# Moving part of batch 1's transposes from TensorE to DMA in an attention and SwiGLU kernel on one core

## The chip, the core and the metric

The program runs on one core of a Trainium2 chip. The core has TensorE for matmuls (PE in the profile, with PEld for its weight loads), VectorE (DVE), ScalarE (ACT), GpSimd (POOL), SyncE (SP) and 16 DMA engines that all of its transfers share. The metric is the device time of one execution in microseconds; less is better.

## The reference

Attention with squared ReLU in place of softmax over 8 batches of 12 heads (448 tokens, head size 64), then a token-wise RMS norm and a SwiGLU layer (768 to 1536 to 768) over all 3584 tokens:

```python
scores = q @ k.transpose(0, 1, 3, 2) / sqrt(64)
attn   = maximum(scores, 0) ** 2 / 448 @ v
x      = attn.transpose(0, 2, 1, 3).reshape(3584, 768)
xn     = x / sqrt(mean(x * x, axis=-1) + 1e-6) * rms_g
g      = xn @ w_gate
out    = (g * sigmoid(g) * (xn @ w_val)) @ w_out
```

Inputs and output are float32 in HBM; the kernel converts to bf16 in the loads and accumulates in float32.

## The kernel before

The kernel writes out its instruction order itself. While the program is built, a small planner (`Planner`) keeps a clock for every engine, gives each operation an assumed cost, and emits the operation that can start first; ties go by a rank. On the chip every engine then runs its instructions in that fixed order and waits on semaphores where data isn't there. The assumed costs change only the order.

**Loads.** GpSimd issues them in the order q and k of batch 0, v of batch 0, four slices each of `w_gate` and `w_val`, q, k and v of batch 1 (each in halves of six heads), two halves of `w_out`, then q and k of batch 2. At most eight of them are in flight: the ninth waits for the first.

**Heads to columns.** Scores need q and k with the head dimension on the partitions (`qkT`, six pairs of heads j = 0 to 5). For batches 0 and 1 (`PE_T = 2`) TensorE transposes them through PSUM (`transposes`, L419 and L427; 16 matmuls for a pair of batch 1) and VectorE copies the result to `qkT` (L437). For batch 2 and later VectorE sorts each chunk of q and k by head (L326) and SyncE issues eight DMA transposes (`transpose_dma`, L339).

**Attention.** For each pair of heads there are score products into PSUM (L483, L501, L519), ReLU on ACT or DVE (L467, L465), a square on DVE (L470), and then, for two pairs at a time, the products with v (L605). ACT scales the result into `xT` (L653). For the norm, DVE squares `xT` and adds into a float32 sum (L668, L670), closes it to one bf16 tile (L674), and one TensorE product with a matrix of ones sums over partitions. ACT makes the reciprocal root with Ln and Exp (L728, L732), which needs another function table than Silu does (L390 loads one), and DVE scales `xT` to `xn` (six instructions, L737). Batch 0 runs in two halves of 224 tokens; its last pairs of heads are already squared by ACT straight from PSUM (L656).

**Stream.** All products of the feed-forward layer go through `Stream.step` (L872). The array is used as two halves of 64 rows: a slot holds one matmul on the upper half for one group (its lead) and one on the lower half for another (its follow). A slot in which only one half has work lasts as long. The feed-forward of one batch (gate and value, `gv`, then the output projection, `o`) is mixed with the attention of the next but one, batch 0's with that of batch 1. When there is no follow, a rule looks for another group to lead so that the pair is full; it holds for batches 1 to 6 only.

**Head.** In the first 26 us, in which data arrives and batch 0's attention runs, the planner puts products on zeros into TensorE's gaps (`fill`, L1147; in the trace the first of these follow each other in 0.187 us, from 8.9 us on in about 0.1). A gap is filled if it is at least 0.3 us long by the plan, up to 0.15 us before its end.

Of the kernel before, what the change touches and what calls it, by code (L numbers as in the profile page):

```python
# [9 lines left out]
BF16 = mybir.dt.bfloat16  # L10
# [56 lines left out]
class Planner:  # L67
# [84 lines left out]
    def run(self, until):  # L152
        while not until():
# [8 lines left out]
            if e == "PE" and self.fill is not None:  # L162
                self.fill(self.free["PE"], t)
            if op == "step":
# [8 lines left out]
def kernel(  # L173
# [104 lines left out]
    def load(nm, b, h0=0, h1=H, deps=()):  # L278
        src = src_of[nm][b, h0:h1]
        if (nm, b) == ("k", 0):  # L280

            def runs_of_seven():
                nc.gpsimd.dma_start(  # L283
                    out=wo_sb[:D, h0:h1, :S], in_=src.rearrange("h (p u) d -> p h (u d)", p=D)
                )

            ops = [pool_dma(0.7, D * U * D * 4 * (h1 - h0) / 1e3, 300.0 if h1 == 2 else 340.0, runs_of_seven, deps)]
            landed.setdefault((nm, b), {}).update({h: ops for h in range(h0, h1)})
            return
# [5 lines left out]
        for prt, n, u0, u1 in parts:  # L295
# [12 lines left out]

            ops.append(pool_dma(0.72, kb, (300.0 if h1 == 2 else 340.0) if b == 0 else 400.0, whole, deps))
        landed.setdefault((nm, b), {}).update({h: ops for h in range(h0, h1)})  # L310
# [5 lines left out]

    def transpose_dma(b, deps, seen):

        jobs = [("k", c) for c in range(UH)] + [("q", c) for c in range(NCH)]
        turned[b] = []  # L320
        sorts = []
        for nm, c in jobs:

            def sort(op, nm=nm, c=c):
                n = (P if c < UH - 1 else D) if nm == "k" else PC
                nc.vector.tensor_copy(  # L326
                    out=sorted_of[nm, b][:n, c, :].rearrange("p (h d) -> p h d", d=D),
                    in_=ld[nm, b][:n, :, c * D : (c + 1) * D],
                )

            sorts.append(add(Op({"DVE": 0.06 + H * D * 0.53e-3}, sort, landed[nm, b][0] + list(seen), rank=6)))
        for nm, c in jobs:

            def turn(op, nm=nm, c=c):
                if b not in qkT:
# [3 lines left out]
                op.ins = nc.sync.dma_start_transpose(  # L339
                    out=qkT[b][:, :, 0 if nm == "k" else 1, at : at + n], in_=sorted_of[nm, b][:n, c, :]  # L340
                ).ins

            need = list(deps) + sorts
            turned[b].append(add(Op({"SP": 0.1}, turn, need, ends=arrives(170, 120.0))))

# [14 lines left out]
    def load_wo(s, n):  # L360
        w = FT // n
        w_in["o", s] = pool_dma(0.85, 2360, 400.0, lambda: nc.gpsimd.dma_start(
            out=wo_sb[:, s * w : (s + 1) * w, :],
# [213 lines left out]
    def attend(b, j, lo, w, due):  # L577
# [40 lines left out]
        def fn(op):  # L618
            op.ps = one.ps
            products(False, op.ps.tile)  # L620
            if b == 0 and j == HP - 2:

                ev = add(Op({"DVE": 0.07 + 2 * w * 1.042e-3}, evict, [op], rank=-1))
                sq = add(Op({"ACT": 0.05 + 2 * w * 0.833e-3}, square_ps, [op], rank=-1))
                plan.take(op.ps.banks, [ev, sq])
                squared[lo, j] = sq
            else:
                ev = add(Op({"ACT": 0.05 + 2 * w * 0.833e-3}, evict, [op], rank=1))
                plan.take(op.ps.banks, [ev])
            if b == 0 and j == HP - 2:  # L630
                pass
# [3 lines left out]
            else:  # L635
                cost = (0.08 + 2 * w * 1.042e-3) * (2 if j else 1)
                sq = add(Op({"DVE": cost}, square, [ev], rank=2))
            if j == HP - 2 and b == 0:
                summed[b, lo] = sq
# [15 lines left out]
        def square_ps(op):  # L655
            nc.scalar.activation(  # L656
                out=xn_of[1][:, j : j + 2, lo : lo + w], in_=me.ps.tile[:, :, :w], func=ACT.Square, scale=inv_attn
            )
# [30 lines left out]

    summed, squared, used = {}, {}, []  # L690

# [67 lines left out]
    class Stream:  # L759
# [14 lines left out]
        def options(self, half, taken):  # L774
            here = self.at[half]
            order = [g for g in self.open if g.n == 1]
            order += ([here] if here in self.open and here.count[half] % KT else []) + self.open
# [21 lines left out]
        def step(self, t):  # L799
            lead = self.pick(0, None, t)  # L800
            follow = self.pick(1, lead, t)
            if lead is not None and follow is None and lead.note and 0 < lead.note[0] < B - 1:

# [124 lines left out]

    def norm_sums(b, lo, w):
        return Group(  # L930
            1, w, lambda i: ones_bf[:], lambda i: accs[b, lo][1][:, :w],
            lambda g: norm_scale(b, lo, w, g), "psSS", lambda i: [Later(summed, (b, lo))],
            False,
        )
# [152 lines left out]
    EARLY = 4  # L1087

    def half_scores(lo, j, due):
        for jj in range(2):  # L1090
# [18 lines left out]
    def attention_full(b):  # L1109
# [4 lines left out]
        for j in range(0, HP, 2):  # L1114
            if b < PE_T:
                transposes(b, j)
# [16 lines left out]

    def fill(t0, t1):
        if not fill_on[0] or t1 - t0 < 0.3:
            return
        s = None
        for x in single[::-1]:
# [19 lines left out]
    for s in range(NSL):  # L1158
        load_w("g", s)
        load_w("v", s)  # L1160
    for nm in ("q", "k", "v"):
        load(nm, 1, 0, 6)
        load(nm, 1, 6, 12)
    load_wo(0, 2)
# [4 lines left out]
    for b in range(B):  # L1169
        groups = ffn(b)  # L1170
        if b == 0:
            stream.add(groups[:24])
            plan.run(lambda: first.end.done < NEVER)
            end_head()
            attention_half(HS)
            attention_full(1)
            stream.add(groups[24:])
# [5 lines left out]
        if b + 2 < B:  # L1183
# [10 lines left out]
            attention_full(b + 2)  # L1194
        if 0 < b < B - 1:
            ready_for_norm(b)
# [41 lines left out]
```

## Time and profile before

| | us |
|---|---|
| Median of three runs (lowest, highest) | 441.63 (439.43, 444.19) |
| The profiled execution | 438.65 |
| Its span in the trace | 436.9 |
| Batch 0's first feed-forward product starts | 26.13 |
| Batch 1's first transpose on TensorE starts | 48.29 |
| Batch 0's first output-projection product starts | 71.76 |
| Batch 1's first gate product starts | 85.96 |
| Batch 2's first score product starts | 94.96 |

A row of the trace gives the start, the time that the group took, the engine, the line of the kernel and the tiles. The profile counts TensorE as busy from the first start to the last end of overlapping matmuls, so a busy TensorE can still run half-empty slots.

### The profile page before, as it was taken

What the parts mean: (1) busy time and instruction counts of PE and PEld (TensorE: products, weight loads), DVE (VectorE), ACT (ScalarE), POOL (GpSimd) and SP (SyncE); (2) the same over time, 40 slices, a digit from 0 to 9 for tenths busy, and PEclk for the clock granted to TensorE, in tenths of its full rate; (3) what the DMA queues carried; (4) which work ended last, traced back from release to release, by engine and by line L of the source; (5) the groups of instructions that cost most, each with busy time, mean ns of one, the idle gap of its engine ahead of it and who ended that gap; (6) DMA issues with size and microseconds to landing.
All of it is one profiled execution on the core that took longest, in us unless ns stands there. A gap on an engine that the chain in (4) does not pass through costs nothing.

```text
span 436.9 us, 17119 instructions
## 1 busy us (share of the span) xinstructions
PE 430.4 (99%) x7836; PEld 350.8 (80%) x7836; DVE 255.6 (59%) x461; ACT 263.9 (60%) x391; POOL 47.1 (11%) x67
## 2 busy tenths in 40 slices
PE   8999999999999999999999999999999999999996
PEld 5577876778778777789978997789988997688865
DVE  2987588638945774685757465676655456432210
ACT  3982496649846765775748665586757666342222
POOL 8522400012012001201200012001000000000000
PEclk9999999999999999999999999999999999999999
DMA  8999995799569747886952999089001300030013
GB/s 105 196 204 202 202 205 74 123 187 119 82 94 165 148 96 96 110 154 121 123 77 74 133 144 125 13 141 159 7 2 47 102 4 3 2 91 22 3 38 110
DMA packets 82680, 44.75 MB, mean 102 GB/s; under 512 B 41904, under 2 KB 79152, under 8 KB 82608
## 3 DMA queue, kind: packets, MB, share of 16 engines
q0 software_dynamic: 43232, 24.38, 41.3%
q1 hardware_dynamic: 38992, 18.94, 21.1%
q8 instruction: 61, 1.00, 0.9%
q10 hardware_dynamic: 384, 0.34, 0.3%
q14 instruction: 11, 0.09, 0.1%
HBM read 48.76 MB, written 11.01 MB: 137 GB/s over the span
## 4 chain that ended last, share of the span: by engine, by line
PE 95%; ACT 1%; DMA 1%; DVE 1%; issue 1%; POOL 0%; POOLq 0%
PE psP L872 77%; PE psS L605 8%; PE psS L483 6%; PE psS L519 1%; DMA wo_sb<-in_k_dram 1%; PE psP L427 1%; PE psS L501 1%; PE psP L1147 1%; ACT r L467 1%; PE psP L419 0%; POOL qb L299 0%; DVE hT L957 0%; PE psP L920 0%; ACT qkT L439 0%; POOL wo_sb L283 0%
## 5 line engine op out<-in xcount | busy, mean ns | idle before, releaser
L872 PE MATMUL psP<-xn,wg_sb 64*64 64x448 bf16 (+1 forms) x2304 | 235.1, 338 | 0.2 <-ACT sil L943 0.2
L872 PE MATMUL psP<-xn,wv_sb 64*64 64x448 bf16 (+1 forms) x2304 | 218.5, 338 | 0.1
L467 ACT ACTIVATE r<-psS 128x896 bf16<-128x896 f32 (+1 forms) x162 | 143.6, 922 | 53.5 <-PE psS L483 28.4
L872 PEld LDWEIGHTS <-wg_sb 64*64 64x64 bf16 (+1 forms) x2304 | 132.3, 105 | 17.5 <-issue 3.0
L872 PEld LDWEIGHTS <-wv_sb 64*64 64x64 bf16 (+1 forms) x2304 | 132.6, 105 | 16.3 <-issue 3.3
L872 PE MATMUL psP<-wo_sb,hT 64*128 64x384 bf16 (+2 forms) x1562 | 139.6, 321 | 0.0
L470 DVE TENSOR_TENSOR r<-r 128x896 bf16<-128x896 bf16 (+1 forms) x165 | 98.7, 616 | 58.7 <-ACT r L467 57.9
L872 PEld LDWEIGHTS <-hT 64*128 64x128 bf16 (+1 forms) x1562 | 100.1, 97 | 23.4 <-issue 3.2
L957 DVE TENSOR_TENSOR hT<-sil,psP 128x448 bf16<-128x448 bf16 (+1 forms) x108 | 61.0, 565 | 58.3 <-PE psP L872 44.5
L943 ACT ACTIVATE sil<-psP 128x448 bf16<-128x448 f32 (+1 forms) x108 | 54.9, 508 | 59.7 <-PE psP L872 55.9
L1017 ACT COPY ost<-psP 128x384 f32<-128x384 f32 (+1 forms) x55 | 25.9, 475 | 43.3 <-PE psP L872 42.8
L483 PE MATMUL psS<-qkT 64*64 64x448 bf16 (+1 forms) x420 | 48.2, 350 | 0.0
L605 PE MATMUL psS<-r,vb 64*64 64x448 bf16 (+1 forms) x716 | 43.7, 335 | 0.3 <-PE psS L605 0.2
L737 DVE SCALAR_TENSOR_TENSOR xn<-xT,g_sb,rstd 128x448 bf16<-128x448 bf16 (+1 forms) x54 | 30.2, 628 | 22.2 <-ACT rstd L732 22.1
L299 POOL DMA_DIRECT2D vb<-in_v_dram x20 | 14.3, 736 | 197.0 <-PE psP L872 189.4
L605 PEld LDWEIGHTS <-vb 64*64 64x64 bf16 x756 | 26.1, 106 | 8.4 <-issue 2.0
L653 ACT ACTIVATE xT<-psS 128x896 bf16<-128x896 f32 (+1 forms) x25 | 21.4, 857 | 9.9 <-PE psS L605 9.9
L483 PEld LDWEIGHTS <-qkT 64*64 64x64 bf16 (+1 forms) x420 | 22.0, 103 | 4.6 <-issue 0.7
L390 ACT ACT_TABLE_LOAD x16 | 20.5, 1283 | 1.0 <-PEq L1222 0.7
L668 DVE TENSOR_TENSOR x<-xT 128x896 f32<-128x896 bf16 x14 | 15.2, 1087 | 3.6 <-ACT xT L653 3.6
L670 DVE TENSOR_TENSOR acc<-acc,x 128x896 f32<-128x896 f32 x14 | 15.3, 1092 | 0.5
L299 POOL DMA_DIRECT2D qb<-in_q_dram x12 | 10.2, 854 | 41.7 <-DVE hT L957 13.0
(61 smaller groups left out, 154.6 us busy)
## 6 DMA issues: line engine op xcount, KB each, us to landing
vb<-in_v_dram POOLq DMA_DIRECT2D x12, 384.0 KB, 6.9
qb<-in_q_dram POOLq DMA_DIRECT2D x6, 672.0 KB, 8.1
out_dram<-ost SPq DMA_DIRECT2D x7, 336.0 KB, 3.0
wg_sb<-in_moe_w_gate_dram POOLq DMA_DIRECT2D x4, 576.0 KB, 15.7
wv_sb<-in_moe_w_val_dram POOLq DMA_DIRECT2D x4, 576.0 KB, 17.3
wo_sb<-in_moe_w_out_dram POOLq DMA_DIRECT2D x2, 1152.0 KB, 14.0
kb<-in_k_dram POOLq DMA_DIRECT2D x6, 384.0 KB, 9.8
out_dram<-ost SPq DMA_DIRECT2D x8, 288.0 KB, 3.2
```

The costliest lines, as they stand in the source:

```text
L299: dma = nc.gpsimd.dma_start(out=stage(nm, b)[prt, h0:h1, : (u1 - u0) * D], in_=src.rearrange("h (p u) d -> p h (u d)", p=n)[:, :, u0 * D : ...
L390: nc.scalar.add_instruction(mybir.InstLoadActFuncSet(name=name, act_func_set_id=n, ins=[], outs=[]))
L467: nc.scalar.activation(out=op.view, in_=src, func=ACT.Relu)
L470: nc.vector.tensor_tensor(out=rl.view, in0=rl.view, in1=rl.view, op=ALU.mult)
L483: nc.tensor.matmul(out=ps[m0:m1, hh, :S], lhsT=qkT[b][prt, j, 0, c * P + m0 : c * P + m1], rhs=qkT[b][prt, j, 1, :], start=True, stop=True,)
L605: mm = nc.tensor.matmul(out=ps[hh * D : (hh + 1) * D, jj, :w], lhsT=vb[prt, 2 * (j + jj) + hh, u * D : (u + 1) * D], rhs=r[prt, hh, :], st ...
L653: nc.scalar.mul(out=to, in_=src, mul=inv_attn)
L737: nc.vector.scalar_tensor_tensor(out=xns[b][:, kt, lo : lo + w], in0=xTs[b][:, kt, lo : lo + w], scalar=g_sb[:, kt : kt + 1], in1=rstd[:, ...
L872: mm = nc.tensor.matmul(out=self.ps[m0:m1, : self.w], lhsT=self.lhsT(i)[prt, m0:m1], rhs=self.rhs(i)[prt], start=(half == 0 and i == 0), s ...
L943: nc.scalar.activation(out=s[:, :w], in_=g.ps[:, :w], func=ACT.Silu)
L957: nc.vector.tensor_tensor(out=hT[:, fb, o : o + w], in0=sil[b, fb, lo][1][:, :w], in1=g.ps[:, :w], op=ALU.mult,)
L1017: nc.scalar.copy(out=to, in_=g.ps[:, :w])
```

## The change

Six things change:

1. Of batch 1, heads 8 to 11 of q and k are loaded first, then heads 0 to 3 and 4 to 7. VectorE sorts heads 8 to 11 into a part of `hT` that isn't used yet, and SyncE issues eight DMA transposes for them. TensorE no longer transposes the pairs j = 4 and 5 of batch 1 (32 matmuls), and VectorE no longer copies them out of PSUM.
2. Batch 1's norm is closed after the second two pairs of heads. The last four heads are squared by ACT from PSUM, VectorE takes over their scaling, and the sum over partitions is three products instead of one.
3. The rule for fuller slots also holds in batch 0's output projection.
4. The function table for Ln and Exp is loaded ahead of batch 1's norm, as it already is for later batches.
5. In the head, between 5.5 and 20 us of the plan's clock, a gap is filled from 0.15 us on, and the fill runs up to 0.05 us short of the planned end, or 0.35 us beyond it ahead of transposes.
6. The planner assumes a lower transfer rate for q and k of batch 0's heads 4 to 7 and for `w_out`.

```diff
-    def transpose_dma(b, deps, seen):
+    def transpose_dma(b, deps, seen, j0=0):
...
+        h0 = 2 * j0
+
+        def ordered(nm, c, n):
+
+            return hT[:n, c + UH * (nm == "q"), S : S + (H - h0) * D] if j0 else sorted_of[nm, b][:n, c, :]
...
                 nc.vector.tensor_copy(
-                    out=sorted_of[nm, b][:n, c, :].rearrange("p (h d) -> p h d", d=D),
-                    in_=ld[nm, b][:n, :, c * D : (c + 1) * D],
+                    out=ordered(nm, c, n).rearrange("p (h d) -> p h d", d=D),
+                    in_=ld[nm, b][:n, h0:, c * D : (c + 1) * D],
                 )
...
                 op.ins = nc.sync.dma_start_transpose(
-                    out=qkT[b][:, :, 0 if nm == "k" else 1, at : at + n], in_=sorted_of[nm, b][:n, c, :]
+                    out=qkT[b][:, j0:, 0 if nm == "k" else 1, at : at + n],
+                    in_=ordered(nm, c, n),
                 ).ins
...
-            if b == 0 and j == HP - 2:
+            if b < PE_T and j == HP - 2:
 
                 ev = add(Op({"DVE": 0.07 + 2 * w * 1.042e-3}, evict, [op], rank=-1))
-                sq = add(Op({"ACT": 0.05 + 2 * w * 0.833e-3}, square_ps, [op], rank=-1))
+                sq = add(Op({"ACT": 0.05 + 2 * w * 0.833e-3}, square_ps, [op] + ([attended[b, lo, "sq"]] if b else []), rank=-1))
...
+            if b and b < PE_T and j == HP - 4:
+                attended[b, lo, "sq"] = sq
+                closed[b] = add(Op({"DVE": 0.08 + w * 1.042e-3}, close, [sq], rank=2))
...
+    def last_squares(w):
+        return x2.bitcast(BF16)[:, :, :w]
...
-            if lead is not None and follow is None and lead.note and 0 < lead.note[0] < B - 1:
+            if lead is not None and follow is None and lead.note and lead.note[0] < B - 1 and (lead.note[0] or lead.note[1] == 'o'):
...
     def norm_sums(b, lo, w):
+
+        def rhs(i):
+            return last_squares(w)[:, i - 1, :] if i else accs[b, lo][1][:, :w]
+
         return Group(
-            1, w, lambda i: ones_bf[:], lambda i: accs[b, lo][1][:, :w],
-            lambda g: norm_scale(b, lo, w, g), "psSS", lambda i: [Later(summed, (b, lo))],
+            3 if b < PE_T else 1, w, lambda i: ones_bf[:], rhs,
...
-            if b < PE_T:
+            if b < PE_T and j < BY_DMA:
                 transposes(b, j)
                 transposes(b, j + 1)
...
-    def fill(t0, t1):
-        if not fill_on[0] or t1 - t0 < 0.3:
+    def fill(t0, t1, late):
+
+        early = 5.5 < t0 < 20.0
+        if not fill_on[0] or t1 - t0 < (0.15 if early else 0.3):
             return
+        if early:
+            t1 += 0.1 + late
...
-    for nm in ("q", "k", "v"):
-        load(nm, 1, 0, 6)
-        load(nm, 1, 6, 12)
+
+    for h0, h1 in ((2 * BY_DMA, H), (0, 4), (4, 2 * BY_DMA)):
+        load("q", 1, h0, h1)
+        load("k", 1, h0, h1)
+    load("v", 1, 0, 6)
+    load("v", 1, 6, 12)
...
             attention_half(HS)
+            transpose_dma(1, [], [], BY_DMA)
             attention_full(1)
...
-        if 0 < b < B - 1:
+        if b < B - 1:
             ready_for_norm(b)
```

In the order of the finished programs, from batch 2 on the slots are the same in number and kind. TensorE has 7842 matmuls instead of 7836: 32 transposes fewer, 25 products on zeros more (81 instead of 56), and for the rest the two extra products of batch 1's norm and another split of slots into 64 or 128 columns.

## The prediction

> **What bounds the kernel now.** I read the page first, for which engine has no slack and where.
>
> ```profile
> PE 430.4 (99%) x7836; PEld 350.8 (80%) x7836; DVE 255.6 (59%) x461; ACT 263.9 (60%) x391; POOL 47.1 (11%) x67
> PE   8999999999999999999999999999999999999996
> ACT  3982496649846765775748665586757666342222
> PEclk9999999999999999999999999999999999999999
> DMA  8999995799569747886952999089001300030013
> ```
>
> TensorE is hardly idle after the head (0.34 us between 40 and 50 us, none from 50 to 95) and its granted clock is full in every slice. So time is won only where TensorE issues less, or where its slots get fuller; a shorter chain on another engine is worth nothing unless TensorE waits for it. DMA is saturated for the first six slices (to 65 us), which is where the new DMA work is put.
>
> Next the chain of waits around the transposes of the pairs 4 and 5 of batch 1:
>
> ```profile
> 62.75 0.19 PE psS L483 x2
> 62.94 0.19 PE psP L872 x3
> 63.13 0.54 PE psP L427 x16
> 63.67 0.29 PE psS L483 x2
> ...
> 68.33 0.54 PE psP L427 x16
> 68.87 1.10 PE psP L872 x20
> ```
>
> These two groups of 16 transposes (L427) are on the chain that ends last, 0.54 us each, with TensorE's own work before and after.
>
> Then the timeline of the norm of batch 1, whose attention ends at 76.8:
>
> ```profile
> 76.80 4.88 PE L872 MATMUL psP<-wo_sb,hT 64*128 64x384 bf16 x54
> 76.92 0.92 ACT L653 ACTIVATE xT<-psS 128x896 bf16<-128x896 f32 x1 [2.74 <-PE psS L605]
> 77.87 1.09 DVE L668 TENSOR_TENSOR x<-xT 128x896 f32<-128x896 bf16 x1 [1.05 <-ACT xT L653]
> 79.00 1.09 DVE L670 TENSOR_TENSOR acc<-acc,x 128x896 f32<-128x896 f32 x1
> 81.53 0.35 PE L872 MATMUL psP<-ssum,ones_bf 64*128 64x448 bf16 x1
> 81.72 0.49 PE L872 MATMUL psP<-wo_sb,hT 64*128 64x384 bf16 x3
> 84.60 3.65 DVE L737 SCALAR_TENSOR_TENSOR xn<-xT,g_sb,rstd 128x448 bf16<-128x448 bf16 x6
> 85.96 0.37 PE L872 MATMUL psP<-xn,wg_sb 64*64 64x448 bf16 x1
> ```
>
> The chain from `xT` to `xn` takes 8 us, but TensorE streams the output projection (`wo_sb,hT`) right through it. Last, busy time by stage (span, PE, PEld, DVE, ACT, POOL, clock, DMA share, GB/s) and the DMA transposes of batch 2 on SyncE's queue:
>
> ```profile
> 50.00:65.00 15.00, 15.00 (x277) 10.96 (x273) 12.31 (x24) 13.70 (x22) 1.76 (x3) 1.00 1.23 208
> ```
>
> ```profile
> 75.32 5.28 SPq L339 DMA_TRANSPOSE qkT<-ks  x4
> 80.64 6.08 SPq L339 DMA_TRANSPOSE qkT<-qs  x4
> ```
>
> **The change, part by part.**
>
> *Transposes off TensorE.* Two groups of 0.54 us leave the chain: -1.08. VectorE's two copies of 0.62 us go too, off the path.
>
> *What replaces them.* Eight sorts on DVE: a sort of twelve heads takes 0.35 us, a third of the elements is at least a third of that, so 8 x 0.12 to 8 x 0.35, 1.0 to 2.8 us. In the program's order they stand between the `hT` products of 43.2 to 47.8 us, where DVE sat idle 0.46 to 0.76 us before each of these. Cost nothing, if the data is there. Before, q's first half of batch 1 landed at 20.82 + 22.6 = 43.4 and the last of k at 48.8. Now q and k of four heads come first: 0.92 MB of float32, where q's first half is 0.69 MB and all of q and k 2.75 MB in the 7.9 us from 40.9 (last slice of `w_val`) to 48.8; so about 43.5. The sorts of k are next at about 44.7. The cover is about 1 us; beyond it DVE stands, `hT` behind it, and TensorE for its bank.
>
> The eight DMA transposes then start near 46. No transpose ran beside loads before, so I bound them: for twelve heads, alone, they are issued in 11.4 us (75.32 to 86.72) and land 2.9 us after issue, so at most 46 + 11.4 + 2.9 = 60.3; with a third of the data, if issue scaled, 46 + 3.8 + 2.9 = 52.7. The first score product of pair 4 came at 64.63 and will come near 64.1 (one transpose group less, a little head). Either way hidden; I take the upper bound, since SyncE's issue time and not the bytes spaced them. They also take DMA time from the loads: in the window of 76 to 88 us the engines were busy 0.75 x 12 = 9.0 us for twelve heads, so 3.0 us for four. Behind them are q and k of heads 4 to 7 (their transposes were at 51.28 and 53.02, the data landed by 48.8), `w_out` (landed 58.4 and 64.0, used from 71.76) and q and k of batch 2 (landed 67.5 to 71.0, sorted from 74.86): covers of 2.5 (of the 3.0 only what falls before 48.8 counts there), 13 and 3.9 us, less 0.5 to 1.1 for the earlier use. POOL issues three loads more at 0.7 us, into a queue that waited 1 to 2.4 us for each place: nothing. SyncE has nothing else until batch 2's transposes.
>
> *Norm, table load and fuller slots.* By the order of the two programs, batch 0's output projection has 65 slots of its own before, six of them half-empty, and 62 after, two half-empty. The row at 76.80 gives a slot: 54 matmuls are 25 pairs and 4 alone, 29 slots in the 4.73 us to 81.53, 0.163 us each. Three fewer is -0.49. But three products for the norm instead of one (each twice, once per half) add slots 448 wide: three more of them in all by the order, at 0.19 (81.53 to 81.72): +0.57. Together +0.08. The chain gets about 4 us shorter (two operations of 1.09 and a table load of 1.28 go, the closing add of 0.62 moves forward), yet what is late next is nothing: from 76.80 to batch 2's first scores at 94.96, 54 slots of 0.163 and 49 of 0.189 make 18.06 of the 18.16 us. No wait was there to be won.
>
> *Head.* 25 more products on zeros at 0.096 us are 2.4 us; TensorE was idle 1.5 us between 5 and 25 us (4.78, 4.39, 4.70 and 4.63 busy of 5 each). So at worst 0.9 late. At best 0.4 early: one copy of 0.83 us leaves ACT for DVE, and DVE trades a ReLU of full size for one of half size. DVE was busy for all of 10 to 20 us and stays the bound there: with the six extra products the transpose of pair 2 comes 0.56 later, at 11.3, and its copy is behind squares that keep DVE until 11.9. I take +0.2, near the middle, and +0.15 because a memset of 0.38 us (0.31 in a row with others, which overlap) now stands right ahead of `xn`, where DVE had 0.16 free. This reaches the end, since TensorE is busy from 26 us on. The lower assumed rates move only the plan.
>
> Sum: -1.08 + 0.08 + 0.2 + 0.15 = -0.65, so 438.65 - 0.65 = 438.0 for an execution like the profiled one. That lies 2.98 below the median of the runs, so 441.0 on the median's scale.
>
> **The rivals.**
>
> *The gain doesn't arrive.* From 50 to 65 us ACT was busy 13.70 of 15 and DVE 12.31. With one transpose group less the same ReLUs must fit 14.5 us: if they set the pace, the score products wait for their banks and the 1.08 comes back as waits of TensorE for L467. With the head's +0.9, 0.08 and 0.15 that is up to +1.1: 439.8, on the median's scale 442.7. For it: ACT had only 1.3 us left. Against: ACT still waited 3.9 us for score products between 50 and 75.
>
> *More than the count.* From 48.29 to 94.96 there are 118 slots of 0.096 us (groups of six start 0.575 apart near 47 us), 73 of 0.163, 49 of 0.189, six transpose groups of 0.54, 21 score groups of 0.19 and three times 0.88 and 0.67 for products with v: 44.4 of 46.7 us. The other 2.3 go to changes between forms. If the new order had none of these, and the head gained 0.4 in place of losing 0.2, it would be a further -2.9: 435.1, or 438.1 on the median's scale. For it: nothing that the order shows, the sequence is much the same.
>
> *Transposes too late (slower).* If, beside the saturated loads, the eight take over 15.2 us from 46 instead of 11.4 (1.9 us each), they land after 64.1 and TensorE stands ahead of pair 4's scores. At twice the time, which a fair share between two queues gives, they land at 46 + 22.8 + 2.9 = 71.7: +7.6, 445.5, or 448.5 on the median's scale. For it: DMA is saturated until 69 us. Against: alone they were spaced by issue, and four heads are a third of the data. [...]
>
> That the change does nothing of what it says is excluded by the program's order: the 32 transposes are gone.
>
> **How the numbers follow.** Forecast 0.5; gain doesn't arrive 0.28; more than the count 0.14; too late 0.08. The runs shown spread by 2.2 to 2.6 around their median, so a median of a few runs may lie 2 either way. Low: the second rival's 438.1 less half such a spread, 437.0. High: the first rival's 442.7 and as much above, 443.9. This leaves out the third rival and the tails of the runs. 1% (4.4 us) is about what a measurement tells from no change. Faster by more than that, below 437.2: the second rival with a low draw of the runs, 0.12. Slower, above 446.0: the third, 0.08. Within: 0.80.
>
> **What would show it.** No L427 near 63 and 68 us; L483 of pair 4 without a wait for a DMA; the eight transposes landed before 61; `w_out` and batch 2's loads up to 3 us later; `xn` of batch 1 some 4 us earlier relative to the end of attention, with TensorE streaming through; batch 0's first gate product between 25.7 and 27.1; from 95 us on the same spacing. The prediction is wrong if TensorE stands still between 45 and 75 us, or if batch 2's first scores come outside 93 to 95.5.

## The result, and the profile after

| | before | after |
|---|---|---|
| Median of 13 runs each (lowest, highest) | 441.20 (438.72, 444.19) | 445.01 (442.87, 446.61) |
| The profiled execution, its span | 438.65, 436.9 | 445.12, 443.3 |
| Mean granted clock of TensorE in it | 1.000 | 0.995 |

The changed kernel is slower: its time is 1.0085 of the time before, 95% interval 1.0059 to 1.0111. The median lies outside the predicted 437.0 to 443.9, and the profile shows both signs that the prediction had named as proof that it is wrong: TensorE stands still between 45 and 75 us, and batch 2's first scores come at 100.98, not between 93 and 95.5.

The page of the changed kernel, first busy time by engine, then TensorE, ScalarE, granted clock and DMA in 40 slices of 11 us:

```profile
PE 432.8 (98%) x7842; PEld 355.4 (80%) x7842; DVE 257.4 (58%) x471; ACT 262.1 (59%) x386; POOL 48.8 (11%) x70
PE   8999996999999999999999999999999999999996
ACT  3783493648955756486657656576757656352212
PEclk9999998999999999999999999999999999999999
DMA  8999999277958976969791899268201300021013
```

The seventh slice (66 to 77 us) is new in three rows: TensorE is down to 6, its clock to 8, DMA is still at 9. Everywhere else TensorE is as full as before.

TensorE's timeline there (start, duration, instructions, and in brackets the idle time ahead and what ended it):

```profile
65.33 0.35 PE L907 MATMUL psP<-xn,wv_sb 64*128 64x224 bf16 x3
70.70 0.56 PE L509 MATMUL psS<-qkT 64*128 64x448 bf16 x2 [5.02 <-DMA qkT<-hT]
...
72.36 0.39 PE L907 MATMUL psP<-xn,wv_sb 64*128 64x224 bf16 x1
...
73.95 0.26 PE L907 MATMUL psP<-xn,wv_sb 64*128 64x224 bf16 x1
```

TensorE has nothing between 65.68 and 70.70. What ends it is the landing of a DMA transpose. Behind it the same `w_val` product takes 0.39 us at 72.36 and 0.26 at 73.95: the granted clock was 0.50 for the first 3.15 us (to 73.85) and 1.00 after them. The stages, with the columns as before (span, PE, PEld, DVE, ACT, POOL, clock, DMA share, GB/s):

```profile
50.00:65.00 15.00, 15.00 (x274) 11.15 (x275) 12.24 (x24) 12.61 (x20) 1.57 (x3) 1.00 1.25 179
65.00:70.00 5.00, 0.68 (x13) 0.45 (x9) 0.96 (x3) 1.50 (x3) 0.00 (x0) 1.00 1.39 192
70.00:75.00 5.00, 4.30 (x50) 3.13 (x50) 2.33 (x5) 2.19 (x3) 0.00 (x0) 0.66 1.28 165
```

In the first window TensorE is busy for all of the 15 us, and ScalarE has 12.61 us of work, less than the 13.70 before: the prediction's first rival, ReLUs that set the pace, is not what happened. DMA moved 179 GB/s where it moved 208. The transposes themselves, by line, with the issue times and the time from issue to landing:

```profile
L360 SPq DMA_TRANSPOSE qkT<-hT x8: 1241/1258/2368, 46.1 to 56.6; - x8
...
  PE psS L509: 5.0, 1
...
DMA to landing us min/median/max: 6.8/9.8/14.0
```

Eight issues, most of them of about 1.25 us, the last at 56.63; it landed 14.0 us later, at 70.6. TensorE waited 5.0 us for it.

The norm of batch 1 did get shorter:

```profile
84.26 0.76 PE L631 MATMUL psS<-r,vb 64*64 64x448 bf16 x12
...
87.26 0.35 PE L907 MATMUL psP<-x,ones_bf 64*128 64x448 bf16 x1
...
90.89 0.37 PE L907 MATMUL psP<-xn,wg_sb 64*64 64x448 bf16 x1
```

From the end of attention (85.0) to the first gate product it is 5.9 us, where it was 9.2 (76.8 to 85.96): 3.3 less, of the predicted 4. TensorE streamed through both, so this gives no time.

By the two profiled executions the account is: head +1.0 (first gate product 26.1 to 27.1), standstill +5.0, half clock +1.5 (measured below), TensorE's own work -1.0 (the predicted -1.08 and +0.08, not measured by itself). Sum +6.5; the spans differ by 6.4. The medians differ by 3.8 only, and why is the second question of the experiments.

### The profile page after: what moved, and what is told of

The parts are those of the page before. It is cut to its first block, busy times and chain, and to the rows that moved or that the text cites. A ratio compares the mean times of both kernels' runs of the same rounds, so it can differ in the third digit from the quotient of the medians.

```text
span 443.3 us, 17156 instructions
## 1 busy us (share of the span) xinstructions
PE 432.8 (98%) x7842; PEld 355.4 (80%) x7842; DVE 257.4 (58%) x471; ACT 262.1 (59%) x386; POOL 48.8 (11%) x70
## 4 chain that ended last, share of the span: by engine, by line
PE 92%; DMA 3%; DVE 2%; SPq 1%; issue 1%; ACT 0%
PE psP L907 74%; PE psS L631 7%; PE psS L509 5%; DMA qkT<-hT 3%; PE psP L1193 2%; SPq L360 1%; PE psS L545 1%; PE psS L527 1%; PE psP L453 1%; PE psP L445 0%; DVE hT L997 0%; PE psP L955 0%; DVE xn L772 0%; DVE acc L496 0%; DVE qkT L463 0%
## 5 line engine op out<-in xcount | busy, mean ns | idle before, releaser
L907 PE MATMUL psP<-xn,wg_sb 64*64 64x448 bf16 (+1 forms) x2304 | 238.0, 339 | 0.3 <-ACT sil L983 0.2
L907 PE MATMUL psP<-xn,wv_sb 64*64 64x448 bf16 (+1 forms) x2304 | 222.4, 339 | 0.1
L907 PEld LDWEIGHTS <-wg_sb 64*64 64x64 bf16 (+1 forms) x2304 | 134.0, 105 | 16.6 <-PE psP L907 3.3
L907 PEld LDWEIGHTS <-wv_sb 64*64 64x64 bf16 (+1 forms) x2304 | 134.0, 105 | 16.1 <-issue 4.2
L997 DVE TENSOR_TENSOR hT<-sil,psP 128x448 bf16<-128x448 bf16 (+1 forms) x108 | 60.9, 566 | 63.6 <-PE psP L907 46.1
L509 PE MATMUL psS<-qkT 64*64 64x448 bf16 (+1 forms) x414 | 49.2, 352 | 5.0 <-DMA qkT<-hT 5.0
L1057 ACT COPY ost<-psP 128x384 f32<-128x384 f32 (+1 forms) x52 | 24.4, 473 | 41.8 <-PE psP L907 41.8
L684 ACT ACTIVATE xT<-psS 128x896 bf16<-128x896 f32 (+1 forms) x24 | 20.5, 853 | 8.6 <-PE psS L631 8.6
L700 DVE TENSOR_TENSOR x<-xT 128x896 f32<-128x896 bf16 x13 | 14.1, 1087 | 1.6 <-ACT xT L684 1.6
L702 DVE TENSOR_TENSOR acc<-acc,x 128x896 f32<-128x896 f32 x13 | 14.2, 1092 | 0.4
```

The lines of the kernel that those rows point to most:

```text
L509: nc.tensor.matmul(out=ps[m0:m1, hh, :S], lhsT=qkT[b][prt, j, 0, c * P + m0 : c * P + m1], rhs=qkT[b][prt, j, 1, :], start=True, stop=True,)
L684: nc.scalar.mul(out=to, in_=src, mul=inv_attn)
L907: mm = nc.tensor.matmul(out=self.ps[m0:m1, : self.w], lhsT=self.lhsT(i)[prt, m0:m1], rhs=self.rhs(i)[prt], start=(half == 0 and i == 0), s ...
L997: nc.vector.tensor_tensor(out=hT[:, fb, o : o + w], in0=sil[b, fb, lo][1][:, :w], in1=g.ps[:, :w], op=ALU.mult,)
L1057: nc.scalar.copy(out=to, in_=g.ps[:, :w])
```

## Experiments

All ratios are to the kernel before, run on the same chip, with a 95% interval.

**Which part: four kernels, two by two.** The change with transposes on TensorE again (and batch 1's loads in the old order), with the old head again, and with both undone.

```diff
-    BY_DMA = 4
+    BY_DMA = HP
...
-            transpose_dma(1, [], [], BY_DMA)
```

> The changed kernel with the transposes of pairs 4 and 5 back on TensorE (and batch 1's loads in the old order); the head's fill, the norm's three products and the fuller slots stay. Theory A, late DMA transposes: no standstill of TensorE between 65 and 71 us, granted clock 1.00 in 70-75, the head's +1.1 us stays; a profile near 438.65 + 1.1 + 0.1 = 439.8, a ratio to the kernel before of 1.000 to 1.004. Rival B, the loss sits in the head and the norm and the standstill only takes up slack: it stays near the changed kernel's ratio, 1.006 to 1.011.

```diff
-        early = 5.5 < t0 < 20.0
-        if not fill_on[0] or t1 - t0 < (0.15 if early else 0.3):
+        if not fill_on[0] or t1 - t0 < 0.3:
...
-        if early:
-            t1 += 0.1 + late
...
-            ops = [pool_dma(0.7, D * U * D * 4 * (h1 - h0) / 1e3, 300.0 if h1 in (2, 8) else 340.0, runs_of_seven, deps)]
+            ops = [pool_dma(0.7, D * U * D * 4 * (h1 - h0) / 1e3, 300.0 if h1 == 2 else 340.0, runs_of_seven, deps)]
...
```

> The changed kernel with the head undone (threshold of 0.3 us for zero products and the old assumed load rates), DMA transposes kept. Theory A: the landing of the last transpose is set by the loads and not by TensorE, so it stays near 70.6; batch 0's first gate product comes 1.1 us earlier (26.0), TensorE stands 1.1 us longer (about 6.1), and the time does not change: ratio 1.007 to 1.010. Rival B, the head's delay adds to the end: 1.1 us less, ratio about 1.006, with a standstill of 5.0 as before.

The third kernel has both edits.

> The changed kernel with both undone (transposes of pairs 4 and 5 on TensorE, old head): only the norm's three products, the early table load and the fuller slots of batch 0's output projection are left of the change. Theory A: the parts that are left count +0.08 us, so the ratio is 0.998 to 1.002, and 1.1 us (0.0025) below the kernel with TensorE transposes and the new head. Rival C, the three products or the earlier closing add cost a wait: ratio over 1.003.

| pairs 4 and 5 by | head | first gate product | pair 4's first scores | median | ratio |
|---|---|---|---|---|---|
| DMA (the change) | new | 27.1 | 70.7 | 445.01 | 1.0085 (1.0059 to 1.0111) |
| TensorE | new | 27.1 | 65.7 | 441.91 | 1.0046 (1.0020 to 1.0072) |
| DMA | old | 26.3 | 69.4 | 445.45 | 1.0118 (1.0081 to 1.0155) |
| TensorE | old | 26.3 | 64.9 | 441.35 | 1.0016 (0.9987 to 1.0044) |

Both kernels with DMA transposes stand still, both without don't. By the ratios the DMA transposes cost 0.004 with the new head and 0.010 with the old, on average 0.007 or 3.1 us; the first row was measured against other executions of the kernel before than the other three. What is left when both are undone (norm, table load, fuller slots) can't be told from nothing, as the predicted +0.08 said.

The 3.1 us are less than the account says, because putting the transposes back also changed what the planner does later. From batch 3's norm product to batch 5's, both kernels with TensorE transposes took 101.5 us, where the kernel before took 100.3 and the two others 100.3 to 100.5; TensorE's order is another there, and it waited for nothing. So some 1.0 to 1.2 us of their time is no price of a transpose. The second row is also a little above its expectation; in its profile TensorE waited 1.3 us for `hT` near 116 to 120, which no other of these profiles has. By the spans the changed kernel is 2.9 us behind it; with these 1.0 and 1.3 us taken out 5.2, where the account gives 5.0 + 1.5 - 1.08 = 5.4.

The wait of the third row:

```profile
69.35 0.56 PE L509 MATMUL psS<-qkT 64*128 64x448 bf16 x2 [4.32 <-DMA qkT<-hT]
```

With the old head TensorE comes 0.65 us sooner, and the last transpose lands 1.35 sooner (it was issued at 55.2 in place of 56.6 and landed 14.0 us later in both), so the standstill is 4.3 and not the 6.1 that I expected: the landing isn't fixed. Part of this was lost again: the clock was at half from 67.2 to 74.0 (0.72 granted in 65 to 70, 0.60 in 70 to 75), so 4.65 us of work ran at half clock in place of 3.15. The time gains nothing from the old head, as expected; the ratio is a little above the expected 1.007 to 1.010.

**Why the transposes land late.** All loads behind q and k of batch 1 are held back until the transposes have landed.

```diff
+                if (nm, b) == ("v", 1):
+                    tc.add_manual_dep(dma.ins, turned[1][BY_DMA].ops[-1].ins.name, behind)
...
-    load("v", 1, 0, 6)
-    load("v", 1, 6, 12)
+    load("v", 1, 0, 6, deps=[crossing])
+    load("v", 1, 6, 12, deps=[crossing])
```

(`crossing` is done when the last transpose is; `w_out` and batch 2's q and k get the same.)

> The changed kernel with the loads of batch 1's v, of w_out and of batch 2's q and k held back until the eight DMA transposes have landed. It will be slow (v is then late for batch 1's first products with v, and w_out for batch 0's output projection), and only the transposes are looked at. Theory A, contention with the loads: once the earlier loads have drained (near 49 us) the transposes land 2.5 to 3.5 us after issue, the last before 61. Rival E, these transposes are slow by themselves (four heads only, from another tile): they land 7 to 14 us after issue and the last near 70. In both the issue on SyncE stays near 1.25 us each if it doesn't depend on the bytes.

The same view of this kernel's transposes:

```profile
L362 SPq DMA_TRANSPOSE qkT<-hT x8: 1235/1244/2092, 46.2 to 56.5; - x8
...
DMA to landing us min/median/max: 2.3/3.0/4.2
```

Same issues, same spacing, landed 2.3 to 4.2 us later in place of 6.8 to 14.0. The loads delayed them; four heads or the tile `hT` didn't. The time of an issue depended neither on the loads nor on the bytes: its median was 1.258 us beside the loads, 1.244 with them held back, and 1.242 (k) and 1.272 (q) for the transposes of twelve heads in the kernel before. The kernel as a whole took 451.9, since v and `w_out` came late.

What loads and transposes moved side by side is in the DMA view of the changed kernel for 52 to 64 us, when `w_out` is loaded (queue, packets, MB, share of 16 engines):

```profile
q0 software_dynamic: 1235, 1.81, 95.4%
q1 hardware_dynamic: 1223, 0.27, 26.2%
```

1235 packets of loads and 1223 of transposes: one for one in this window. A load packet took 148 ns (0.954 x 12 us x 16 / 1235), a transpose packet 41 (0.262 x 12 us x 16 / 1223), and the two overlapped in part (the shares add up to 121.6%): a pair took 12 us x 16 / 1229 = 156 ns of an engine's time. At this rate all 2048 packets of the transposes take 2048 x 156 ns / 16 = 20.0 us, an estimate from these counts. They moved from 50.2 to 68.2, 18.0 us, and the last landing came at 70.6. In the held-back kernel, with the first issue at 46.2 in place of 46.1, the first packets moved between 47.0 and 47.5, so the start was late as well; no run shows why, and none shows why the packets went one for one.

**Small packets beside them.** Then loads with small packets should delay them less. Batch 2's q and k go ahead of `w_out`.

```diff
-    load_wo(0, 2)
-    load_wo(1, 2)
...
+            if b == 0:
+                load_wo(0, 2)
+                load_wo(1, 2)
             transpose_dma(b + 2, last, seen)
```

> The changed kernel with the two loads of w_out issued behind batch 2's q and k instead of ahead of them. Packet theory: beside small packets (those of batch 1's q and k took 56 ns where w_out's took 148) a turn of one packet each is about 16 x 4000/1687 + 39 = 77 ns on an engine where it was 156, so the 128 turns of each engine take 10 us in place of 20, the issue on SyncE (to 57.9) is the limit again, and the last transpose lands before 64: no standstill ahead of pair 4's scores, full clock, 6.5 us less: ratio 0.994 to 0.998. Byte theory (the transposes get a fixed share of saturated engines): they land near 70 as before, standstill 4 to 5 us, ratio 1.006 to 1.011. Rival: w_out, now 7 us later (second half near 73), is waited for by the output projection at 73: up to 3 us come back there, ratio 1.000 to 1.004.

The second kernel has the smaller head change of the last group below.

> The same with the smaller head change (the new assumed load rates and 0.4 us of zero products ahead of transposes, threshold 0.3 us and no 0.1 us more), which measured 0.9971 alone. Packet theory: the TensorE work after the first gate products is 0.7 us less than in the kernel before, so 0.9971 - 0.0015: ratio 0.993 to 0.997. Byte theory: 1.004 to 1.010.

1.0091 (1.0063 to 1.0119) and 1.0065 (1.0033 to 1.0097): no gain in time. Both lie in the ranges of the byte theory, but not for its reason: the landing did move the way of the packets. In the first kernel it took 7.3/8.5/9.2 us from issue (min/median/max), the last transpose landed at 66.5 in place of 70.6, and pair 4's scores waited for no DMA. But TensorE stood elsewhere, and what it waited for was VectorE:

```profile
PE psP L907 <- DVE hT L997: 1.9, 2, 1.7
PE psS L631 <- DVE r L496: 1.6, 1, 1.6
```

and VectorE in turn stood for loads:

```profile
61.28 0.36 DVE L347 COPY qs<-qb 112x768 bf16<-112x768 bf16 x1 [3.02 <-DMA qb<-in_q_dram]
...
67.66 0.36 DVE L347 COPY ks<-kb 128x768 bf16<-128x768 bf16 x1 [3.02 <-DMA kb<-in_k_dram]
```

The sorts of batch 2 now stand early in VectorE's order, where the plan thinks their data is there; the loads came later than that (whether the transposes slowed them isn't shown by itself), VectorE stands 3.0 us twice, and squares and `hT` behind it. After the wait for the squares (`r`, until 62.2) TensorE's clock was also at half, from 62.7 to 66.1 (0.77 granted in 60 to 65, 0.89 in 65 to 70). The transposes' packets moved till 65.3 in place of 68.2. How many of them moved is in the same DMA view as above, 52 to 64 us:

```profile
q0 software_dynamic: 2959, 1.43, 122.0%
q1 hardware_dynamic: 1767, 0.39, 46.1%
```

Beside small packets it is no longer one for one: 1767 packets of transposes against 2959 of loads, six to ten, though transposes waited (each landed 7 us or more after its issue). So the size of the load packets explains a part of the delay, and one for one was measured only beside the large packets of `w_out`; my landing before 64 needed both in full. Why no more packets of the transposes moved isn't shown.

**The price of the half clock.** 26 products on zeros (4.9 us) ahead of pair 4's first scores.

```diff
+            for _ in range(26 if (b, j, c) == (1, 4, 0) else 0):
+                nc.tensor.matmul(out=ps[:, 0, :S], lhsT=ones_bf[:], rhs=busy_bf[:], start=True, stop=True)
```

> The changed kernel with 26 products on zeros (4.9 us) right ahead of the first scores of pair 4, where TensorE stood 5.0 us. Clock theory: the granted clock stays 1.00 from 65 to 75 us, the scores start at the same 70.7 (set by the DMA transposes), and the 1.6 us at half clock are won: profile near 443.5, ratio 1.004 to 1.006. Rival: the low clock was not from the standstill, or the rest of the way to the end waits for something else: no gain, ratio 1.008 to 1.011.

```profile
66.05 5.09 PE L507 MATMUL psS<-busy_bf,ones_bf 128*128 128x448 bf16 x26
71.07 0.36 PE L511 MATMUL psS<-qkT 64*128 64x448 bf16 x2
...
73.03 0.95 PE L633 MATMUL psS<-r,vb 64*64 64x448 bf16 x16
```

From the scores to the first product with v it is 1.96 us at full clock (1.00 granted from 65 to 75); in the changed kernel it was 3.45 (70.70 to 74.15). So the half clock cost 1.5 us there. The ratio, 1.0092 (1.0056 to 1.0128), shows no gain and lies in the rival's range. In this execution the last transpose had landed at 69.1 already, so the zeros, which ran until 71.1, held the scores back themselves, by 2.0 us; and the first gate product was 0.4 late (27.5). The price is shown at its place, a gain in the total is not.

**Planning for the late landing.** If the planner knows, TensorE can do other work.

```diff
-        crossed[0] = max(crossed[0], t + 3.6) + 1.1
+        crossed[0] = max(crossed[0], t + 3.6) + 2.7
```

> The changed kernel with the planner's assumed landing of the DMA transposes put at 2.7 us each instead of 1.1 (the last at about 70.5 instead of 58), so that it puts gate and value products of batch 0 ahead of pair 4's scores. Theory A: the transposes land where they did (near 70.6), TensorE does not stand, its clock stays full, and the 5.0 us of standstill and the 1.6 us at half clock are gone: a profile near 445.1 - 6.6 = 438.5, ratio 0.998 to 1.001. Rival D, the scores of two pairs pushed together then wait for ReLUs on ScalarE and VectorE: up to half of it comes back, ratio 1.002 to 1.006.

The same with 2.5 and the old head:

> The changed kernel with the old head and with the planner's assumed time of the DMA transposes at 2.5 us each: pair 4's scores stand behind more gate and value products of batch 0, about where the transposes landed with the old head (69.4), and batch 1's own gate and value products keep their full slots (the 2.7 us each of the run before made many of them half-empty). Theory A: TensorE stands at most 1 us near 69 us, at full clock after it; against the old-head kernel 3.5 us of standstill and the 1.6 to 2 us at half clock are won: ratio 0.998 to 1.003, where it had 1.0118. Rival D, late scores cost what they save whatever the slots do: ratio 1.007 or more.

The first: 1.0107 (1.0067 to 1.0146), above both ranges. There is no standstill at 70 us and the clock is full,

```profile
65.00:70.00 5.00, 5.00 (x96) 3.46 (x92) 2.99 (x7) 2.91 (x7) 0.00 (x0) 1.00 1.76 174
70.00:75.00 5.00, 5.00 (x72) 3.73 (x70) 3.71 (x7) 3.55 (x5) 0.00 (x0) 1.00 1.34 169
```

yet the gain went away later: TensorE waited 1.2 us for v of batch 2 and 0.7 for VectorE near 103 to 113, and by the program's order 40 of batch 1's gate and value products stand alone in a slot, where 8 did: 16 slots more of 0.189, 3.0 us. These 4.9 us and a first gate product 0.8 later (27.9) leave 0.8 of the 6.5 us won; by the spans it is 0.85 (443.35 to 442.50). The second has full slots and 1.0044 (1.0016 to 1.0072), 0.007 better than its counterpart with the early plan (1.0118). That lies between the ranges of the two theories: most of what theory A promised came, but not all. Its profile has no standstill there and full clock (1.00 granted from 40 to 85), but the two late pairs press ReLUs and squares together, and the products with v wait for them:

```profile
79.80 0.38 PE L631 MATMUL psS<-r,vb 64*64 64x448 bf16 x4 [0.55 <-DVE r L496]
80.33 0.38 PE L631 MATMUL psS<-r,vb 64*64 64x448 bf16 x4 [0.15 <-DVE r L496]
81.13 0.56 PE L631 MATMUL psS<-r,vb 64*64 64x448 bf16 x6 [0.42 <-DVE r L496]
```

**The head.** The new head alone, on the kernel before:

> The kernel before with the new head alone (zero products from gaps of 0.15 us between 5.5 and 20 us, and the changed assumed load rates); from the first products of batch 0's feed-forward on, TensorE's order is that of the kernel before. If the head's delay reaches the end whole: batch 0's first gate product 1.0 us later (27.1), the same spacing after it, profile 439.7, ratio 1.001 to 1.004. Rival: the delay is taken up by waits later in the head or the first batch: ratio 0.998 to 1.001.

0.9991 (0.9964 to 1.0018): the first gate product is 1.25 us later (27.4), the profiled execution 440.38 in place of 438.65, and the medians don't differ. The runs gave a hint: those of the kernel before on the same chip spread from 438.6 to 443.4, these only from 439.3 to 441.7. So the kernel before was profiled three times more.

> The kernel before, unchanged, for another profile: its runs fall in two groups, 438.1 to 440.2 and 440.8 to 443.4, and the profile shown is of the lower group, while the kernel with the new head alone lies between, 439.3 to 441.7. Theory H: the groups are made in the head, where the old head leaves TensorE idle and its clock falls in some executions: a profile of 441 or more shows a granted clock under 1.00 between 5 and 25 us and the first gate product 2 us later than 26.1. Rival: the upper group waits for late transfers in a later batch: the first gate product near 26.1 to 26.6 and gaps of TensorE of some 2 us in all after 60 us.

> The kernel before again, for the same question: which of the two groups it falls in, and whether an execution of 441 or more has its extra time in the head (first gate product near 28, clock under 1.00: theory H) or in gaps after 60 us (the rival).

> The kernel before a third time, for the same question and with the same expectations.

They took 439.71, 441.89 and 441.52. The stages of the head in the first and in the second of them:

```profile
10.00:15.00 5.00, 4.24 (x114) 3.04 (x114) 4.65 (x9) 4.59 (x7) 3.11 (x4) 1.00 1.37 187
15.00:20.00 5.00, 4.71 (x74) 2.77 (x69) 5.00 (x10) 4.38 (x8) 3.28 (x4) 1.00 1.35 203
```

```profile
10.00:15.00 5.00, 3.28 (x69) 2.21 (x68) 3.10 (x6) 2.85 (x5) 3.10 (x4) 0.79 1.33 180
15.00:20.00 5.00, 5.00 (x82) 3.42 (x76) 4.43 (x8) 3.29 (x5) 3.48 (x5) 0.53 1.36 200
```

The kernel before has two heads. With full clock its first gate product comes at 26.1 (26.2 here); in the other, TensorE stands still near 11 us (1.72 us, from 10.43 to 12.15), the granted clock is 0.50 from 12.9 to 19.7, and the first gate product comes at 29.5 (29.2 in the third, with the clock at 0.50 from 13.8 to 20.7). Behind the head these two stay 2.9 to 3.4 us behind the profile of before, to the end. The first has no such delay; of its 1.06 us over that profile, 0.87 are one stop of TensorE at 97.3, for which the profile shows no cause. The profile that the prediction rests on was of the full-clock kind. Theory H holds, and the executions without a profile agree: of the 52 against which the head alone and the three kernels below were measured, the 20 with a mean granted clock of 0.998 or more took 438.6 to 440.2, the 32 below that 440.3 to 443.4. In other groups a few executions at full clock were long too (up to 443.5).

Which part of the new head holds the clock:

```diff
-            ops = [pool_dma(0.7, D * U * D * 4 * (h1 - h0) / 1e3, 300.0 if h1 == 2 else 340.0, runs_of_seven, deps)]
+            ops = [pool_dma(0.7, D * U * D * 4 * (h1 - h0) / 1e3, 300.0 if h1 in (2, 8) else 340.0, runs_of_seven, deps)]
...
```

> The kernel before with the changed assumed load rates alone (old rule for zero products): 5 zero products more than the kernel before, six of them now ahead of the scores of pair 2. If the rates' new order holds the clock and the extra zero products pay the 1 us: one group of runs, 438.5 to 440.5, ratio 0.995 to 0.999. If the zero products hold the clock: two groups as in the kernel before, ratio 0.998 to 1.002, spread over 3 us.

The new rule of `fill` with the old rates:

> The kernel before with the new rule for zero products alone (gaps from 0.15 us, 0.1 us over the gap and 0.4 more ahead of transposes, from 5.5 to 20 us) and the old rates: 15 zero products more than the kernel before. If the zero products hold the clock: one group of runs, near 440, ratio 0.997 to 1.000. If the rates do: two groups, both about 1 us above those of the kernel before, ratio 1.001 to 1.004.

The new rates, and 0.4 us ahead of transposes only:

> The kernel before with the changed rates and 0.4 us of zero products more ahead of the transposes, threshold 0.3 us as before: 13 zero products more than the kernel before, where the whole new head has 25. If a part of the zero products is enough, one group of runs at 439 to 440.5, ratio 0.995 to 0.999; if not, two groups with a spread over 3 us.

| on the kernel before | zero products | first gate product | runs | executions with a mean clock under 0.998 | ratio |
|---|---|---|---|---|---|
| nothing | 56 | 26.1 to 29.5 | 438.1 to 444.2 | 32 of 52 | 1 |
| rates | 61 | 28.6 | 439.2 to 446.4 | 4 of 12 | 0.9986 (0.9960 to 1.0012) |
| rule of `fill` | 71 | 26.8 | 438.7 to 443.6 | 2 of 12 | 0.9983 (0.9954 to 1.0013) |
| rates, 0.4 ahead of transposes | 69 | 27.1 | 438.9 to 442.0 | 1 of 12 | 0.9971 (0.9949 to 0.9993) |
| whole new head | 81 | 27.4 | 439.3 to 441.7 | 0 of 12 | 0.9991 (0.9964 to 1.0018) |

The profile with the rates alone (of its longest execution, 446.4, and read for the head only) has the clock at 0.75 from 10 to 15 us; in those with 69 or more zero products it is 1.00. So the more zero products, the rarer the low clock: 69 to 71 held it in most executions (11 and 10 of 12), 81 held it in all twelve. Whether the new order by the rates helps beside them isn't shown. The price is a later first gate product, 26.8 to 27.4 where it was 26.1. The intervals overlap, so the order of the last three is not shown; the kernel with 69 is the only one whose interval lies below 1, and only just.

**What is left of the change without DMA transposes.** New head, fuller slots and early table load on the kernel before, without the three products.

```diff
-            if lead is not None and follow is None and lead.note and 0 < lead.note[0] < B - 1:
+            if lead is not None and follow is None and lead.note and lead.note[0] < B - 1 and (lead.note[0] or lead.note[1] == 'o'):
...
-        if 0 < b < B - 1:
+        if b < B - 1:
```

> The kernel before with the new head, the fuller slots of batch 0's output projection and the early table load, without DMA transposes and without the norm's three products. By the order TensorE's work after the first gate products is 0.26 us less than in the kernel before, and the head alone measured 0.9991: ratio 0.996 to 1.001 if the parts add, with a profile near 440.1 and few runs above 441. Rival: the early table load or the new choice of slots opens a wait: ratio 1.001 or more.

1.0015 (0.9989 to 1.0041), in the rival's range, but the interval holds the other too: no gain to be measured. In its profile TensorE stood twice for 0.5 us, at 146.8 and 153.7, with no cause that the profile shows; whether slots or table load cost the little that it lies above the head alone isn't shown.

## Why the prediction was wrong

The step that failed is "Either way hidden; I take the upper bound". It bounded the landing at 60.3 with rows of transposes that ran alone: 11.4 us of issues and 2.9 from issue to landing. The issues took 11.78, close to the bound; from issue to landing it took up to 14.0, since the loads delayed the transposes' packets, and the cover of 4 us was gone.

The third rival had the place and the cause (the loads), and its 71.7 for the landing and 445.5 for an execution like the profiled one stand against 70.6 and 445.12. That the price is so near is partly luck. It doubled the issues, which were not slowed, in place of the time to landing; its 7.6 us of standstill were 5.0, because TensorE came to pair 4's scores at 65.7 and not at 64.1; and it had neither the 1.5 us of half clock nor the late head. Its factor of two, "a fair share between two queues", is shown by no run: the transposes landed 6.8 to 14.0 us after issue where it was 2.3 to 4.2 with the loads held back, and from 52 to 64 us the loads moved 1235 packets to 1223 of theirs beside `w_out`, and 2959 to 1767 with `w_out` last. It got 0.08 because I weighed "a third of the data" against "DMA is saturated", when what counted beside the large packets of `w_out` was the number of packets. The trace of before had them: 5632 packets of DMA transposes between 75 and 88 us, nearly all of a batch, so some 1900 for four heads (2048 in the end), each of which could wait for a packet of `w_out`.

The rest by the prediction's steps:

- *Transposes off TensorE, -1.08.* They are gone at 63 and 68 us. With +0.08 for slots and norm this closes the account of the profiles to 0.1 us; neither was measured by itself.
- *Sorts, 1.0 to 2.8 us in VectorE's gaps, at no cost.* They took 1.75 us between 44.86 and 47.4. ScalarE waited 1.6 us for one of them, TensorE never.
- *Loads up to 3 us later.* The two halves of `w_out` landed at 61.4 and 70.3 in place of 58.4 and 64.0, 3.0 and 6.3 later. Batch 2's q and k came 4.8 to 6.1 later (73.6 to 76.7). So most of the delays are about twice the bound. TensorE waited for none of these loads: its first product with `w_out` came at 77.75, after the standstill.
- *A stall costs its length.* The prediction priced waits by their length alone. This one cost 1.5 us more, for the clock (0.50 from 70.45 to 73.86).
- *Head, +0.2 of -0.4 to +0.9, and +0.15.* By profiles of a head at full clock it was +1.0 to +1.8 (first gate products at 27.1 to 27.9): at or beyond the worst bound, not near the middle. Why beyond, no run told apart. By medians it was nothing, since the new head also removes the half clock.
- *438.0, which "lies 2.98 below the median of the runs, so 441.0".* The offset was taken to stay with the change. Most of it belonged to the old head: its median mixed two kinds of execution, and the profile was of the quicker. The changed kernel's profiled execution is 0.1 from its median. This error has the other sign: on the profiles the change costs 6.5 us, on the medians 3.8.
- *The same spacing from 95 on.* From batch 4's first scores to the end it holds to 0.2 us.

## What to carry to other kernels

How quick a DMA is by itself does not bound how late it lands beside a saturated queue: here 2.3 to 4.2 us after issue with the loads held back, and 6.8 to 14.0 beside them. As an estimate, count its packets, and price each with one packet of the queue that it shares the engines with; here that was near beside large packets (20.0 us, where they moved in 18.0), and too short beside small ones (a landing before 64, where it was 66.5). An experiment that puts one part of a planned order back can move the rest of the order too: compare the stretches that the edit should not touch. When the median lies well above the profiled execution, look for a second kind of execution before carrying the offset over to another kernel. A wait moved away from TensorE by a new plan comes back where the plan's other assumptions no longer hold: here as half-empty slots, as late squares, and as VectorE standing ahead of a load.

## What the hardware showed beyond that

- TensorE's granted clock fell to 0.50 after gaps shorter than the 5.02 us of the changed kernel too, and the length of a gap did not decide it alone. It fell after one gap of 1.72 us in the second extra profile of the kernel before (10.43 to 12.15), after 1.63 us of standstill with `w_out` last (60.59 to 62.22), with 1.60 us of idle time between 10 and 15 us with the rates alone, and in the third extra profile after 0.87 us of idle time between 10 and 12 us and 0.44 between 13 and 14. It stayed at 1.00 through 1.78 us (65.80 to 67.58) in the kernel with `w_out` last and the smaller head change.
- The stretches at half clock in these traces lasted 3.41 us in the changed kernel (70.45 to 73.86) and about 3.4 with the rates alone and with `w_out` last, and about 6.8 in the two extra profiles (12.9 to 19.7 and 13.8 to 20.7) and in the changed kernel with the old head (67.2 to 74.0). Besides, the last 0.8 us of the changed kernel's span were at half clock, after TensorE's last work; in the profile of before there was no stretch at half clock. How much work fell into a stretch depended on when it began: 3.15 us in the changed kernel, 4.65 with the old head.
- Loads and transposes together moved fewer bytes than loads alone: 179 GB/s in the changed kernel where the kernel before moved 208 between 50 and 65 us, with the DMA share at 1.25 and 1.23.
